# One static work order for another in a fused attention and feed-forward kernel

## The chip, the core and the metric

The program runs on one core of a Trainium2 chip. The metric is the device time of one execution in microseconds (us); smaller is better. The core has engines with instruction queues of their own: TensorE (PE, matmuls; its weight loads are shown as PEld), VectorE (DVE), ScalarE (ACT), GpSimd (POOL) and SyncE (SP). An engine takes its instructions strictly in the order in which the program lists them and waits where an input or a buffer is not ready; transfers are issued from the queues of POOL, SP and ACT and run on 16 shared DMA engines.

## What is computed

The reference, cut to what matters (8 batches, 12 heads, 448 positions, head size 64; 3584 tokens, model width 768, hidden width 2048):

```python
scores = np.matmul(q, k.transpose(0, 1, 3, 2)) / np.sqrt(64)
attn   = np.maximum(scores, 0.0) ** 2 / 448
x      = np.matmul(attn, v).transpose(0, 2, 1, 3).reshape(3584, 768)
h      = x @ w_in
out    = (0.5 * h * (1.0 + erf(h / np.sqrt(2)))) @ w_out
```

## The kernel before, in words

The work is cut into some 1480 operations, each a closure that emits the instructions of one engine. Attention is done batch by batch, in three groups of four heads. Per group of a batch the operations are:

- loads of q, k and v, cast to 16 bits on the way, issued by POOL (add_q, add_k, add_v, lines 546 to 577); the weights come the same way (add_win, add_wout). In the built program the loads of POOL take eight semaphores in turn, so a load is issued only when the eighth before it has landed;
- the transposes of q and k. Batches 0 and 1 do them on PE through PSUM (add_tk, add_tq, lines 600 and 625), and DVE or ACT copies the result out. From batch 2 on they are DMA transposes issued by SP (add_T_dma, lines 655 to 708; the instruction is on line 663), one for k and one for q of each group, and DVE or ACT then fills the other half of the q tile with two copies (fill_halves). SP's queue is in order, and it also issues the stores of the output;
- seven QK blocks (add_steps, line 752 for the matmuls): PE multiplies into one of three PSUM buffers, ACT or DVE takes the relu of it (lines 764 and 766), DVE squares it (line 773). In batch 0 a block is half as wide, and two go together;
- one AV (add_av, line 813), and two copies of its result x out of PSUM (line 514 on DVE, 516 on ACT).

Then follows the feed-forward part: the first product F1 (line 865, followed by the gelu on ACT, line 875) and the second (line 1182). Four batches' F1 and all of the second product are done in seven instead of eight block products, with sums formed on DVE; the F1 of that kind is line 1009. F1 of batch 0 needs the attention output of batch 0 and the weight block of its column. PE's queue weaves these products between the attention of later batches. At the end stands the last block of 128 output rows: its last piece of PSUM is filled in two parts of 256 and 128 columns, each with an addition on DVE (line 1216) and a store (line 1143) issued from the ACT and the SP queue.

A matmul of the QK and AV kind works on quarters of PE's array (64 by 64, four at a time), one of the feed-forward kind on the whole array (128 by 128). One QK block is four matmuls, an AV 28, an F1 word 6 (or 12 half as wide), a second product 8.

What order these operations have is not decided at run time. The string ORDER (lines 83 to 171) lists them all. A word is a letter for the engine (P for PE, A for ACT, D for DVE, G for POOL, S for SP) and the number of the operation; words of one letter, read in turn, are the queue of that engine. Z1024 and Z672 are matmuls on zeros that write to a scratch buffer. place() takes the words one by one:

```python
for word in ORDER.split():
    if word[0] == "Z":
        op, eng = next(fills), "PE"
    else:
        op, eng = self.open[int(word[1:])], names[word[0]]
```

and run() then emits the closures in that order, with waits wherever an operation needs the result or the buffer of another. The planner's estimates in the file no longer decide anything, since ORDER holds every operation.

POOL has gates besides: a tiny copy that reads a transposed q tile (add_gate, line 712; add_vgate, line 720) and so keeps all later loads of that queue back until that transpose has landed.

Words that matter below, with the size that lands in the core's memory:

| words | what |
|---|---|
| G0 G3, G1 G4 G7, G2 G5 G6 | batch 0: rest of k (224 KB each), rest of q (112, 112 and 336 KB), v (224 KB each) |
| G117 G118 G119, G121 G122 G123, G125 G126 G127 | batch 1: k, q, v of groups 0, 1, 2, 224 KB each |
| G8, G9 | w_in columns for F1 words m=0,1 and m=2,3: 384 KB each, three issues |
| G120, G124, G128 | w_in for m=4 to 7, 8 to 11, 12 to 15: 768 KB each, three issues |
| G238, G239, G241 | w_out: 1536 KB (one issue), 768 KB (two), 768 KB (two) |
| G147 G148, G150 G151, G153 G154 | batch 2: k and q of groups 0, 1, 2, 224 KB each |
| G149 G152 G155 | batch 2: v, 224 KB each |
| S228 S229, S231 S232, S234 S235 | batch 2: DMA transposes of k and q, of groups 0, 1, 2 |
| P99 | the last AV of batch 0 |
| P141, P143 | F1 of batch 0: m=0,1 and m=2,3 on the first half |
| P294 and P309 | a QK of batch 2, group 0 and group 1: the first of their groups in the order after |

Of the kernel before, what the change touches and what calls it, by code (L numbers as in the profile page):

```python
# [106 lines left out]
D452 P504 P539 P541 D458 A475 A505 A463 G422 A540 G424 D482 D506 A542 P489 P471 D464 G425 P513
D472 P543 P525 A514 D455 P477 D449 S407 A478 P468 A544 A469 D572 D490 A526 P507 P483 D479 D484
P545 S552 A508 A470 D485 G560 P519 S554 P501 A546 P486 P498 D502 S555 G563 D570 P521 A520 A487
P527 A522 A528 P529 S557 P549 A499 A530 D491 P533 P495 D553 A550 D488 A534 S445 D473 D556 P613  # L110
A496 D509 S558 D476 D614 P492 D493 P634 A494 A635 P616 D617 G426 D503 D571 P531 P523 P625 D500
A532 P628 P510 P535 D618 D626 A524 A511 A536 D497 D515 D573 A629 P547 G566 D512 A548 P576 P574
D615 D559 P646 P619 G561 A647 P516 S446 D575 G562 P622 D620 S714 G564 D577 A623 P640 G565 A517
D641 D624 P578 P580 A518 D627 A579 P537 A538 P637 D636 P610 D621 D648 D581 A611 D642 D630 P676
D638 P584 S715 D612 S717 P582 D585 G567 A677 A716 D583 G568 D639 P649 D592 P661 P631 S718 D590
A662 P586 D632 P643 D591 A650 P788 A633 D587 A644 G723 A789 P652 D663 A653 D651 P596 P670 P658
D719 P594 P673 D645 A671 S720 D654 A595 P655 D659 G726 S721 G569 G729 P667 D660 D597 D656 A674
D672 A668 P776 P598 P600 A657 S588 P664 A777 G724 D678 P779 D675 D601 A599 S845 D722 P797 D593
P602 D669 A798 A780 P604 D778 A665 D603 P785 P791 A786 A792 D666 D605 P839 P606 D840 G725 P679
P773 P800 D841 A774 D787 D607 P700 D680 A801 P712 G727 A681 A701 D781 D790 D733 P809 P782 S846  # L120
P833 A713 A783 P682 P688 D775 A683 A810 D793 G728 D784 D847 P686 S848 S849 G730 G731 G854 A834
P836 P821 D850 P794 A689 A822 D799 P806 D837 S851 A687 P830 P704 A795 A807 D735 D796 S852 A831
P696 P815 A705 A697 P803 D808 P812 A813 P692 P698 G857 D811 D802 A693 P710 D832 P824 A816 D804
D814 G732 A699 P896 A825 D805 D817 P818 D897 G860 G855 D823 P890 P827 A711 A819 P702 D891 D835
A828 G856 D829 A820 A703 P926 D838 S956 G858 P902 P884 A903 A885 D826 G859 D853 P694 A927 D734
P684 P923 D924 A685 P893 A894 P842 A695 P914 P887 P708 P690 A843 S957 A888 D958 A915 P947 D895
P917 A844 A709 D898 A691 S589 D892 G861 D886 D928 S608 P899 A948 A900 P706 A918 S609 S959 P737
D736 P920 D889 P908 D904 D901 P905 G862 A738 D921 D922 P938 S960 D906 A909 A707 P911 A912 D961
D916 P739 P935 A907 D913 D740 P974 P741 A939 A975 P992 A742 D925 P932 A936 D940 P743 D949 P745
D919 A993 D744 D910 P950 A933 D755 D746 P977 D753 P929 S962 D754 A951 P944 P747 A978 P749 A930  # L130
A945 A931 P1004 P1001 D952 S963 D934 A1005 D748 P941 P757 D937 A942 D750 P759 D946 S751 D979 D756
A1002 D943 G1481 D964 P968 A758 P980 P953 D1037 A981 D760 P983 P763 P761 D984 P971 A969 D970 D764
A954 P1007 D985 D976 A762 D1003 D1045 D1046 P767 A972 A955 G863 A1008 D768 P765 P965 P998 P995
A966 P868 P1022 D973 A999 D1006 D766 A869 D982 D967 S752 D1038 A996 A1023 P986 D1041 P989 D997
P872 P1025 D987 A990 A988 D1047 D994 P1016 A1026 P1031 P769 A1017 D991 D1009 A1032 P1019 D1000
P1010 D770 P1028 A1020 P1049 A1029 P1066 D1033 P1051 A1067 D864 P1068 D1040 D865 P1070 A1011 A1012
D1024 P1013 D1039 P870 A1071 D1048 A1050 D1069 A1014 D1052 D1117 P1053 D1042 P1072 A1054 D1044
P1055 D1073 P1057 P1074 D871 D1056 P1083 D866 S771 D1075 P1100 P1060 P874 A873 D1043 P1077 D1058
P1063 A1059 D1018 P1080 D1078 D1015 A1084 P1087 D1061 D1030 D1081 D1064 P876 D1021 A1101 P1085
A1088 P1102 D1027 A1065 D1103 A1082 P1104 P1034 D1086 D875 A1105 D1035 D1036 P1089 A1079 P1106  # L140
P1091 P1108 P1121 D1107 D1090 P1111 P1138 P1094 A1062 D1118 A1122 D1092 P878 D1112 A1093 D1095
D1109 D867 D877 D879 P1125 D1119 P1123 A1139 A1076 D1341 P1114 P1097 A1096 A1113 P1142 D1098 P1140
A1110 P880 D1115 D1124 P1155 A1099 A1126 D1120 D1141 A1116 P1172 A1143 P1144 D881 D1145 P1193
D1189 D1229 P1127 A1173 D1190 P1157 A1156 S772 P1174 D1191 D1175 P1149 P1195 P1178 A1194 D1150
D1128 P1176 D1158 D1342 P1132 D1133 P1161 P1159 P1129 D1179 P1146 A1160 D1162 D1192 D1196 P1197
P1183 A1177 P1163 P1166 D1130 P1135 D1164 P1169 D1167 A1131 D1147 A1148 D1136 P1199 S882 A1151
D1184 D1230 P1152 A1165 A1198 P1180 D1170 P1201 D1200 P1233 D1181 S883 D1153 P1250 A1251 D1231
A1234 P1186 D1187 P1235 P1252 D1343 D1232 D1202 A1185 D1236 A1182 A1154 A1188 P1241 P1203 A1137
A1168 D1253 A1134 P1258 P1256 A1171 D1204 D1209 P1205 D1257 D1206 P1254 D1210 P1239 P1213 P1215
D1212 A1214 D1259 D1240 D1216 P1264 D1211 P1244 P1261 D1262 D1245 D1242 S1207 P1219 P1217 D1220  # L150
P1267 A1218 D1265 P1247 P1223 P1221 D1248 D1224 P1284 D1344 A1268 P1269 D1222 D1270 P1225 A1285
P1237 P1286 D1301 A1266 P1288 D1226 P1273 P1271 P1305 A1255 S1208 A1238 D1287 D1274 D1306 P1345
D1302 A1289 P1290 A1272 D1291 P1275 P1362 D1276 D1303 P1278 A1260 P1309 P1295 D1296 P1307 D1279
P1292 A1346 D1308 D1293 P1347 P1364 D1348 D1310 P1281 P1298 P1351 D1282 S1227 A1277 A1363 D1299
# [1369 lines left out]
```

## Time and profile before

| | |
|---|---|
| time of three runs | 366.73, 366.67, 365.64 us; median 366.67 |
| span of the profiled execution, first to last instruction | 363.4 us |
| PE busy in that span | 355.2 us |
| DVE, ACT, POOL busy | 297.0, 216.4, 64.3 us |
| moved by DMA | 42.97 MB |

The profile is one execution. Its own time is its span; the median of the runs lies 3.3 us above it, which is what surrounds the first and the last instruction. A page shows the busy time of each engine, then the span in 40 slices with a digit for the busy tenths, then the DMA queues (q0 is POOL's, q1 SP's), the chain of work that ended last, and the costliest groups. Further views list instructions in order of time (timeline), busy time by stretches (windows) and groups by shape.

### The profile page before, as it was taken

The numbers are of one execution on the slowest core, as the hardware profiler recorded it, in microseconds if no ns is written. First come the engines' busy times: TensorE is split into PE (matmuls) and PEld (weight loads), VectorE is DVE, ScalarE is ACT, GpSimd is POOL, SyncE is SP. The second block draws the span as 40 slices with busy tenths as digits, with TensorE's granted clock in tenths as the row PEclk, the third lists the DMA queues.
The fourth block names the chain that finished last, engine by engine and source line by source line (L and its number), as shares of the span: only waits on it lengthen the run. The fifth ranks groups of instructions, "written<-read, shape, count | busy, mean of one in ns | idle before, by whom it ended". The sixth has DMA issues, their size and how long they took to land.

```text
span 363.4 us, 8571 instructions
## 1 busy us (share of the span) xinstructions
PE 355.2 (98%) x3589; PEld 224.7 (62%) x3589; DVE 297.0 (82%) x518; ACT 216.4 (60%) x345; POOL 64.3 (18%) x104
## 2 busy tenths in 40 slices
PE   8899999999999999999999999999999999999995
PEld 4566565455545455544445556988887788778663
DVE  3998886598988999999889999989788657656862
ACT  5997674688778649779898678346143244116200
POOL 8665700432401403224010000000000000000000
PEclk9999999999999999999999999999999999999999
DMA  9999999999999899999695211003002020302232
GB/s 176 200 201 204 201 205 180 178 187 178 168 169 176 142 144 169 213 161 188 128 196 78 88 45 43 2 3 88 1 2 87 18 73 0 87 5 85 88 88 87
DMA packets 72326, 42.97 MB, mean 118 GB/s; under 512 B 37984, under 2 KB 68960, under 8 KB 72288
## 3 DMA queue, kind: packets, MB, share of 16 engines
q0 software_dynamic: 32912, 22.47, 43.2%
q1 hardware_dynamic: 38736, 19.46, 26.4%
q8 instruction: 28, 0.46, 0.5%
q10 hardware_dynamic: 640, 0.51, 0.4%
q14 instruction: 10, 0.08, 0.1%
HBM read 45.61 MB, written 11.01 MB: 156 GB/s over the span
## 4 chain that ended last, share of the span: by engine, by line
PE 92%; ACT 3%; DVE 2%; DMA 1%; issue 0%; DVEq 0%
PE pso L1182 35%; PE psh L865 21%; PE pb L1009 18%; PE ps L752 10%; PE pav L813 8%; ACT a_sq L764 2%; DMA k<-in_k_dram 1%; DVE a_sq L773 1%; ACT qT L516 1%; DVE qT L514 0%; PE tp L608 0%; PE tp L636 0%; DVE a_sq L766 0%; DVE kT L514 0%; DVE xT L514 0%
## 5 line engine op out<-in xcount | busy, mean ns | idle before, releaser
L764 ACT ACTIVATE a_sq<-ps 128x896 bf16<-128x896 f32 (+1 forms) x133 | 116.1, 922 | 22.0 <-PE ps L752 21.5
L773 DVE TENSOR_TENSOR a_sq<-a_sq 128x896 bf16<-128x896 bf16 (+1 forms) x169 | 97.2, 614 | 3.0 <-ACT a_sq L764 2.5
L865 PE MATMUL psh<-xT,win_sb 128*128 128x448 bf16 (+1 forms) x420 | 77.2, 337 | 0.0
L1046 DVE TENSOR_TENSOR part<-pb,part 128x448 f32<-128x448 f32 x80 | 47.0, 618 | 18.1 <-PE pb L1009 16.5
L865 PEld LDWEIGHTS <-win_sb 128*128 128x128 bf16 x420 | 38.9, 98 | 36.0 <-issue 8.5
L1182 PEld LDWEIGHTS <-s_sb 128*128 128x128 bf16 x456 | 43.3, 98 | 28.9 <-issue 3.8
L752 PE MATMUL ps<-qT,kT 64*64 64x448 bf16 (+1 forms) x756 | 48.3, 337 | 1.7 <-ACT a_sq L764 1.0
L1182 PEld LDWEIGHTS <-h_sb 128*128 128x128 bf16 x336 | 31.9, 98 | 22.3 <-issue 3.8
L875 ACT ACTIVATE h_sb<-psh 128x448 bf16<-128x448 f32 x64 | 34.8, 551 | 18.2 <-PE psh L865 17.9
L766 DVE TENSOR_SCALAR a_sq<-ps 128x896 bf16<-128x896 f32 (+1 forms) x36 | 38.5, 1073 | 7.2 <-PE ps L752 6.7
L1182 PE MATMUL pso<-wout_sb,s_sb 128*128 128x384 bf16 (+2 forms) x232 | 41.1, 321 | 0.0
L1182 PE MATMUL pso<-wout_sb,h_sb 128*128 128x384 bf16 x224 | 41.0, 326 | 0.0
L1182 PE MATMUL pso<-t_sb,s_sb 128*128 128x384 bf16 x224 | 41.0, 326 | 0.0
L1009 PEld LDWEIGHTS <-win_sb 128*128 128x128 bf16 x384 | 36.8, 98 | 3.6 <-issue 0.7
L813 PE MATMUL pav<-a_sq,v_sb 64*64 64x448 bf16 (+1 forms) x756 | 36.5, 329 | 0.3 <-ACT a_sq L764 0.2
L1055 ACT ACTIVATE h_sb<-part 128x448 bf16<-128x448 f32 x48 | 24.7, 572 | 17.7 <-DVE part L1046 17.7
L752 PEld LDWEIGHTS <-kT 64*64 64x64 bf16 x756 | 19.0, 105 | 24.3 <-issue 18.3
L1216 DVE TENSOR_TENSOR osb<-pso,p_sb 128x384 f32<-128x384 f32 x42 | 23.3, 554 | 12.3 <-PE pso L1182 7.6
L1009 PEld LDWEIGHTS <-ws 128*128 128x128 bf16 x288 | 27.7, 98 | 1.3
L813 PEld LDWEIGHTS <-v_sb 64*64 64x64 bf16 x756 | 21.1, 107 | 11.4 <-issue 1.4
L1009 PE MATMUL pb<-xT,win_sb 128*128 128x224 bf16 x192 | 23.0, 259 | 0.0
L516 ACT COPY part<-pb 128x448 f32<-128x448 f32 x16 | 8.2, 531 | 24.7 <-PE pb L1009 24.7
(62 smaller groups left out, 316.1 us busy)
## 6 DMA issues: line engine op xcount, KB each, us to landing
nk<-in_k_dram POOLq DMA_DIRECT2D x23, 224.0 KB, 7.7
nq<-in_q_dram POOLq DMA_DIRECT2D x21, 224.0 KB, 8.7
v_sb<-in_v_dram POOLq DMA_DIRECT2D x5, 672.0 KB, 9.0
out_dram<-osb SPq DMA_DIRECT2D x7, 336.0 KB, 2.8
v_sb<-in_v_dram POOLq DMA_DIRECT2D x9, 224.0 KB, 7.9
out_dram<-osb SPq DMA_DIRECT2D x7, 288.0 KB, 2.9
out_dram<-osb SPq DMA_DIRECT2D x8, 240.0 KB, 3.0
win_sb<-in_moe_w_in_dram POOLq DMA_DIRECT2D x8, 192.0 KB, 8.7
```

The lines of the kernel that those rows point to most:

```text
L752: nc.tensor.matmul(ps[64 * j : 64 * j + 64, e, x * w : x * w + w], kT[r, g, i * 128 + 64 * j : i * 128 + 64 * j + 64], moving, start=True, ...
L764: A.activation(ar, ps, AF.Relu, scale=c_att)
L766: V.tensor_scalar(ar, ps, c_att, 0.0, op0=mybir.AluOpType.mult, op1=mybir.AluOpType.max,)
L773: V.tensor_mul(box["a2"][:, :, :used], ar, ar)
L813: nc.tensor.matmul(pav[0][o2 : o2 + 64, e, :w], vt[b][r, 2 * g + e, bass.ts(i, D)], box["a2"][r, y, o : o + w], start=(i == 0), stop=(i == ...
L865: nc.tensor.matmul(ph[:, x * n : x * n + n], win_sb[:, kd, bass.ts(m + x, 128)], xT[b][:, kd, c], start=(kd == 0), stop=(kd == KD - 1),)
L875: A.activation(h_ring()[:, m : m + nm, o + c.start : o + c.stop], box[0][:, :S].rearrange("p (x n) -> p x n", x=nm), AF.Gelu,)
L1009: nc.tensor.matmul(bank[name][:, y, z * HS : z * HS + HS], w[:, k, bass.ts(mm, 128)], right()[:, k], start=first and k == 0 and z == 0, st ...
L1046: V.tensor_add(get(to), ps(name), get(other))
L1055: A.activation(h_ring()[:, m : m + 2, o + half[c].start : o + half[c].stop], src().rearrange("p (x n) -> p x n", x=2), AF.Gelu,)
L1182: nc.tensor.matmul(box[bank][:, n0:n1], left()[:, kf], right()[:, kf, n0:n1], start=bool(need) and kf == 0, stop=kf == K2 - 1, skip_group_ ...
L1216: V.tensor_add(out()[:, n0:n1], box[bank][:, n0:n1], other()[:, n0:n1])
```

## The change

Only ORDER is replaced; every operation of the one list is in the other. 42 operations go from DVE to ACT and 40 from ACT to DVE (relus, copies out of PSUM, fills). All engines get another sequence: PE's from the fourth word on; POOL's from the eighth, up to the batch 3 loads; SP's within the transposes of batches 2 and 3. The list after has three lines fewer, so that line numbers after it are smaller by three.

On POOL, the loads of batch 2 (G147 to G155) come ahead of parts of the weights and of batch 1's v: the sequence is now ... G8 G126 G120 G124 G151 G148 G119 G128 G127 G147 G150 G9 G123 G238 G239 G154 G155 G241 G240 G153 ..., where it was ... G126 G5 G8 G122 G120 G124 G119 G128 G123 G9 G127 G239 G238 G241 G147 G148 G150 G151 G153 G154 .... On SP the six transposes of batch 2 come as S232 S229 S228 S235 S231 S234 instead of S228 S229 S231 S232 S234 S235. PE changes between the attention kind of matmul and the feed-forward kind 89 times instead of 103. Batch 2's first QK stands 14 F1 words after P99 instead of 27. The two parts of the last piece swap places: P1470 (128 columns) now comes ahead of P1469 (256 columns), while their stores keep the order S1476 (256 columns), S1477.

The diff, cut to the lines that are spoken of:

```diff
@@ -81,88 +81,85 @@
 
 
 ORDER = """
-G0 G1480 D13 A10 A16 P14 D15 G1 P11 D12 P17 P36 P33 D18 G3 P19 D20 P21 A37 D22 A34 P39 P42 G4 P23
-P51 D43 P25 P48 A40 P54 A52 D24 D26 G7 G118 A55 P66 D44 Z1024 Z672 P63 A67 D49 D35 D41 A64 P69 D53
-G2 P57 P27 D28 D65 P31 A58 D32 D38 D68 P75 P78 P131 P29 A70 D132 A76 G117 P102 G121 P45 D59 A79
-A103 G6 P129 P111 A112 P108 D71 G125 A109 P105 A46 D30 P133 D130 A134 D77 D106 D56 P72 P96 A47
-P159 A73 P137 D50 A97 D74 G126 A160 P174 P84 G5 P139 P60 D80 D138 A175 G8 G122 A85 D113 G120 P81
-D104 P156 D61 D62 G124 A82 D98 D110 D83 D86 G119 P93 P90 P141 D107 A94 P162 A157 P87 A91 G128 P114
-G123 A142 A163 A88 P135 D95 D140 D92 P99 D115 D89 A116 D100 P165 G9 A136 P171 P145 D166 A172 P195
-P180 G127 D101 D167 P198 P251 A146 P249 D173 D196 G239 A252 P253 A199 D158 G238 P222 A181 P213
-G241 D164 D161 A250 P168 A223 P243 G147 A254 D169 S228 A214 D176 D170 P257 P189 P177 P183 D190
-P219 D220 A244 A258 G148 A178 P263 A179 A264 P255 D184 D182 D191 G150 P186 D185 P207 G151 P192
-A256 P267 D224 D200 P265 A193 A268 D221 D194 P143 A266 G153 S229 D208 S231 P261 P204 A187 A144
-D215 A262 D209 P210 A205 P216 D197 S232 P247 D188 P259 A248 A211 A260 G154 D206 D217 D218 P201
-D212 D202 P225 G237 S234 P245 A203 A226 A227 A246 P366 P364 A367 G240 D380 G149 D388 A365 P368
-A369 P352 P372 A353 A373 P356 S235 D383 D381 G152 D384 G155 A357 G242 D387 D389 P378 A379 P348
-A349 D382 P354 D230 A355 G269 D385 D233 P370 A371 P362 P358 P291 A363 A292 P294 A295 P285 A359
-G270 D286 P360 S408 P279 A361 P276 D277 P309 P350 A280 A310 A351 P374 P282 D236 A375 G271 S409
-D296 D287 D281 P318 S411 A283 P288 P376 D289 D284 P392 P312 P300 A377 A319 D391 A313 D293 D278
-A393 A301 G272 D386 G273 P339 P394 P396 P315 G274 D390 D290 D395 A340 D316 P306 D302 G417 D317
...
-D1436 D1440 P1443 D1442 P1445 D1444 P1447 D1455 D1446 P1449 D1453 D1448 S1451 P1457 D1454 D1450
-S1452 P1459 D1456 D1458 P1461 D1460 P1463 D1462 S1473 P1465 D1464 P1467 D1466 S1474 P1469 D1468
-S1475 P1470 D1471 S1476 D1472 S1477
+G0 G1480 Z672 D13 P14 D15 A10 P11 D12 A16 P17 D18 P33 A34 P36 P42 D43 G1 P21 D22 G3 G4 G7 G118 G117
+P19 D20 P39 G2 G125 A37 D44 P23 D24 A40 D38 P54 A55 P51 A52 P25 D26 P48 D49 Z1024 P66 A67 G122 G6
+P27 D28 G121 G5 G8 P57 A58 P69 A70 D35 P31 P131 D32 P63 D50 P108 G126 A109 G120 D68 D132 D41 A64
+G124 P29 D30 P75 P129 D130 P102 P45 A76 P137 D53 A103 D59 D56 A46 A47 P111 P78 A112 A79 G151 G148
+P84 A85 P135 P174 A175 G119 D71 D65 P72 A73 A74 D138 P105 D110 D80 P133 D106 P96 A97 D77 P159 A160
+D86 P60 D61 P81 P90 D62 D134 A82 D83 G128 G127 P93 A94 P141 P156 D113 A91 A142 D107 P171 A172 D104
+P87 A88 A89 D92 P139 D98 P114 G147 S232 A157 S229 S228 D95 D136 D140 P99 D100 A115 A116 D161 A101
+P165 G150 G9 G123 P145 G238 G239 G154 D173 S235 S231 A166 P222 P183 D184 P162 A223 A163 D185 A146
+P249 P186 A250 P207 D176 A208 P168 D169 P255 A256 P257 A258 P253 A187 P204 A254 P213 A214 D164 D170
+D167 D158 P177 A178 G155 D224 D205 G241 D206 P216 G240 G153 A217 P180 S234 D181 A179 P251 A252 D218
+P198 A199 D188 D200 P219 P195 P243 G271 A244 P267 D196 D220 D221 A268 P263 A264 P210 A211 D212 P192
+P189 P265 P143 D197 A266 D182 D209 A144 P259 A190 D215 P247 A260 D193 D194 G269 G270 G242 P261 S409
+P225 G149 G237 A230 D191 A262 D226 A248 P294 A295 P201 D227 P291 A202 A203 P285 D380 A292 P245 A246
+P366 D388 A367 A286 P364 A365 D287 D381 P368 A369 P352 P372 A353 A373 P356 A357 D389 D391 D382 P378
+D233 A379 P348 A349 D296 P362 A363 P279 A280 P309 A310 D236 D383 G152 G272 G273 P276 A277 P354 P360
+A355 A361 P318 D384 D281 P282 P288 D283 D289 G274 P370 A371 D293 A319 P374 P312 A375 D278 D320 D284
+P300 A301 D302 P339 S411 D390 D290 A313 D314 P358 D386 A359 P350 A351 P376 A340 S408 S412 S414 P315
+P306 A307 P297 S415 P324 G417 G420 G275 D316 A377 P303 D410 A325 D311 P392 A393 P394 A298 G423 G418
+D308 G419 D387 D385 A304 P396 D395 D397 D317 P333 P336 A299 P330 D334 A337 P398 D399 P400 A331 D305
+D401 P402 P456 D403 S406 A413 D457 P342 D326 D427 A343 D332 P321 P327 A322 A323 S551 D428 A328 D344
+P447 D341 P404 P431 P453 D405 A448 D432 P450 A451 P465 A466 D335 A454 D458 P433 D429 D434 D467 D329
+G421 P435 A436 P437 D338 P462 D430 P459 A463 D460 D461 D438 P345 A346 P480 G422 D416 G424 G425 A347
...
+A1422 A1372 P1425 D1426 P1427 D1428 S1431 P1429 A1412 A1361 A1375 A1409 A1392 A1355 D1433 D1434
+D1430 P1437 A1438 D1435 P1439 D1436 P1441 D1440 D1442 P1443 D1444 S1432 P1445 D1446 P1447 D1453
+D1454 D1448 P1449 D1450 D1455 S1451 D1456 S1452 P1457 A1458 P1459 D1460 P1461 A1462 S1473 P1463
+P1465 D1464 P1467 D1466 P1470 D1472 D1468 S1474 S1475 P1469 D1471 S1476 S1477
 """
```

More of the change, by code (lines that the diff above doesn't have):

```diff
@@ L107 @@
[L107 to L154, printed above, removed]
@@ new lines @@
+P483 P439 P441 D449 A481 P471 D440 A484 D485 A472 D442 P489 S407 S552 A553 S554 D464 D452 S555 P513
+A514 D455 P443 D444 D490 D491 P539 P541 P477 D478 D479 G560 A540 P507 A508 P468 A542 P474 P504 A505
+A469 D556 A470 S557 S445 G563 D482 P545 A546 S558 D475 P525 A526 P486 D487 D488 P498 A499 D473 P501
+A502 P543 P519 D476 P495 A496 A520 P613 D572 D614 P492 A544 D493 D570 A494 D509 P634 D635 P616 A617
+P521 P549 G426 A522 A550 P625 D571 D626 G566 P510 A511 D506 P628 A629 D503 P529 A530 D512 P527 G561
@@ new lines @@
+A528 S446 G562 S714 S715 G564 S717 G565 S718 P533 P531 P646 G567 D627 D500 D515 A647 G568 A534 G723
+A532 D497 P619 D620 P516 P640 D517 D518 D621 D648 D615 P622 G726 P547 A548 A641 D716 D630 P523 A524
+A623 P535 A536 D636 P574 A575 P576 D573 P637 A638 D559 S720 P610 P673 P578 A674 D642 D577 D611 A579
+D624 P580 D581 P537 A538 P584 S721 A722 D639 P582 D612 P649 G569 G729 G724 P670 D618 D592 D585 D650
+A671 P631 A632 A633 P652 P643 D583 D651 D590 D591 P586 D587 P594 G725 P676 A653 D654 D675 P664 A644
@@ new lines @@
+D645 A595 P788 A665 P596 D789 D593 A677 P658 P667 A668 D659 P655 G727 P661 G728 D790 P776 A777 S588
+D669 D597 P598 D662 D663 P600 D672 D666 A656 A657 A599 A719 S845 S846 P602 D678 P785 A786 D601 D603
+P779 A780 D660 D778 P797 P604 A798 D605 S848 S849 P606 P839 G730 D787 P791 G731 A792 P679 A680 D607
+D840 P773 A774 P800 D793 A681 D801 D850 D775 P712 D802 G854 P700 A713 A701 P833 A834 P782 P809 D781
+D783 P682 A683 D784 P688 A689 A810 D733 D799 P686 A687 P836 D837 P821 A822 P794 A795 P806 A807 D823
@@ new lines @@
+D847 P830 D796 A831 D838 D832 P696 A697 P704 A705 P803 D735 P815 D816 D808 A804 P812 A813 P692 A693
+P698 P710 A711 P896 S851 S852 P824 D814 A825 A699 D805 D811 D817 P818 A819 D897 P827 A820 G857 G732
+D853 D828 P890 D835 A891 D892 P702 D841 A703 P902 P926 G860 G855 A927 D928 G856 D829 G858 P884 A903
+A885 G859 P684 P694 D826 D886 A685 P893 P923 A924 P842 D894 S956 S957 D895 P887 D888 A695 D904 A843
+A844 P899 A900 P708 P911 A709 P947 D889 A948 A912 P914 A915 D958 S589 S608 S609 S959 P690 P706 A707
@@ new lines @@
+D901 P917 P920 A921 S960 G861 G862 D898 D734 P905 A691 D918 D919 D925 P974 A975 D736 D976 P932 D913
+A906 D961 A907 P737 A738 A933 P739 D740 G1481 D934 D922 P938 A939 P908 A909 P935 A936 D910 P741 A742
+D916 P743 D744 P950 D951 D952 S962 P977 D949 A978 P929 P941 A942 D943 P944 A945 D979 A930 A931 P745
+D746 S963 A964 D940 P747 D748 S751 D937 P980 A981 D753 D754 P1001 A1002 P992 A993 P749 P757 A758
+D750 D755 D1003 D946 P759 P965 A966 P1004 D1005 P953 D954 D955 D760 P968 A969 D970 P989 A990 D991
@@ new lines @@
+P761 D982 P983 P971 G863 D1045 A762 P1028 A972 P763 D764 A984 D967 P868 D973 D756 D985 A1029 P767
+D1037 P995 P998 A996 D768 D869 D997 D1046 D1048 P986 A987 A988 D994 P1022 A1023 P765 D766 P872 A999
+D1000 D1006 D1024 P1007 A1008 D1009 D864 D865 P1025 A1026 S752 P1016 A1017 P769 S771 D770 P1031
+A1032 D1038 P1010 D1041 P1019 A1020 P1013 A1014 D1011 A1012 P870 D871 P1049 P1066 A1067 D1047 P1083
+D1040 D1044 A1050 P1051 D1052 D866 P1070 A1071 P1068 P1053 P1100 A1054 D1039 D1042 P1055 D1056 P1057
@@ new lines @@
+D1058 A1084 P1087 A1101 P1104 A1105 A1059 A873 D1069 A1088 P1060 D1043 P1074 D1018 P1072 D1027 D1073
+D1075 D867 D1061 A1062 A1076 P1063 D1064 P1085 P1102 D1086 P874 D875 P1077 P1080 D1081 P876 P1089
+D1103 A1082 P1091 P1108 P1106 D1090 P1094 D1092 A1093 D1078 A1079 D1119 P1121 D1107 D1109 A1122
+D1015 P1097 P1111 D1112 A1113 P1138 A1139 A1110 D1095 D877 D1117 P1114 S772 D1098 D1115 P1125 P1155
+P1172 D1021 A1156 D1030 P880 D881 D1231 P1142 D1033 D1229 A1116 P878 A1126 P1034 A1143 D1118 D1120
+A1173 P1123 D1124 P1140 D1141 A1035 D1230 D879 A1036 P1157 D1158 P1174 D1175 P1176 P1159 A1160 A1177
@@ new lines @@
+P1127 D1341 P1161 D1128 P1144 D1162 A1099 P1178 D1179 D1145 P1166 D1167 P1163 P1180 P1149 A1065
+P1183 D1181 A1096 D1189 P1186 P1193 S882 D1164 P1169 D1150 P1132 D1184 D1187 A1188 D1342 P1233 D1133
+D1191 P1250 A1251 A1134 D1170 P1129 P1146 A1234 A1185 D1232 P1235 P1252 A1171 D1147 A1148 P1152
+D1190 P1195 D1253 D1130 D1236 D1153 P1256 D1257 P1239 D1240 P1135 D1136 D1344 P1261 D1262 P1244
+D1245 A1194 D1196 P1241 P1258 D1259 P1254 P1267 P1197 A1198 D1242 P1264 P1247 P1199 D1265 P1284
+A1154 A1285 A1268 D1200 A1165 A1131 D1248 P1201 A1182 A1137 D1202 P1269 P1286 A1168 D1287 P1203
@@ new lines @@
+P1290 P1271 D1192 P1205 A1151 D1209 D1211 D1210 D1204 P1237 P1213 S883 S1207 D1206 D1214 P1215 P1217
+D1216 P1219 S1208 D1291 D1212 A1218 P1221 D1220 D1222 P1223 P1225 A1260 A1238 A1255 D1270 A1272
+P1288 A1289 D1224 S1227 D1226 P1295 P1273 P1275 P1292 A1246 D1301 D1296 P1345 P1362 A1346 D1274
+D1276 P1278 P1281 A1277 D1293 D1279 A1363 A1280 D1343 D1282 P1366 A1297 A1249 P1349 P1347 P1364
+D1348 P1298 P1351 D1303 P1305 A1306 D1365 P1368 D1299 A1300 D1302 D1304 D1352 P1353 P1370 P1356
+D1369 P1373 D1371 D1357 P1376 A1266 P1307 D1354 P1359 S1228 D1374 D1308 P1379 A1380 D1377 A1243
```

18 lines of the change are left out of this document (5 added, 13 removed).

## Prediction

> **What bounds the kernel now.** I read the page first, then the windows, then PE's timeline.
>
> ```profile
> span 363.4 us, 8571 instructions
> ...
> PE 355.2 (98%) x3589; PEld 224.7 (62%) x3589; DVE 297.0 (82%) x518; ACT 216.4 (60%) x345; POOL 64.3 (18%) x104
> ...
> PE 92%; ACT 3%; DVE 2%; DMA 1%; issue 0%; DVEq 0%
> ```
>
> ```profile
> 10.00:20.00 10.00, 8.57 (x224) 5.99 (x225) 9.97 (x19) 9.92 (x16) 5.84 (x9) 1.00 1.32 201
> ...
> 20.00:30.00 10.00, 9.29 (x230) 6.88 (x225) 9.01 (x20) 9.69 (x14) 5.71 (x9) 1.00 1.29 203
> 30.00:40.00 10.00, 10.00 (x108) 5.45 (x106) 7.67 (x13) 7.02 (x12) 7.25 (x12) 1.00 1.30 202
> ...
> 50.00:60.00 10.00, 10.00 (x101) 5.74 (x100) 7.97 (x11) 5.63 (x11) 0.73 (x1) 1.00 1.33 201
> ```
>
> The columns are stretch, length, then busy us of PE, PEld, DVE, ACT and POOL, clock, DMA share, GB/s. Two stages differ. Up to about 30 us DVE and ACT are both full and PE waits for them; after that PE has no gap, at full clock. So a new order can gain in two ways alone: a shorter opening, or less PE time per unit of work later. Any wait that it adds on PE after 30 us is paid in full, since no later idle time takes it up.
>
> A busy PE still spends time on something other than streaming:
>
> ```profile
> 39.84 2.44 PE L865 MATMUL psh<-xT,win_sb 128*128 128x448 bf16 x12
> 42.22 0.76 PE L752 MATMUL ps<-qT,kT 64*64 64x448 bf16 x12
> ...
> 94.35 0.76 PE L752 MATMUL ps<-qT,kT 64*64 64x448 bf16 x12
> 95.05 1.47 PE L1182 MATMUL pso<-wout_sb,s_sb 128*128 128x384 bf16 x8
> 96.36 1.46 PE L1182 MATMUL pso<-t_sb,s_sb 128*128 128x384 bf16 x8
> 97.75 0.38 PE L752 MATMUL ps<-qT,kT 64*64 64x448 bf16 x4
> 97.96 1.49 PE L813 MATMUL pav<-a_sq,v_sb 64*64 64x448 bf16 x28
> 99.29 0.36 PE L752 MATMUL ps<-qT,kT 64*64 64x448 bf16 x4
> 99.80 0.38 PE L752 MATMUL ps<-qT,kT 64*64 64x448 bf16 x4 [0.15 <-ACT a_sq L764]
> ```
>
> Read start to start. An AV takes 99.29 - 97.96 = 1.33 us, so four such matmuls 0.19. A second product takes 1.31 ahead of one of its kind (95.05 to 96.36) and 1.39 ahead of a QK (96.36 to 97.75): 0.08 for the change to quarter-array matmuls. Three QKs take 0.70 ahead of a product (94.35 to 95.05) where 3 x 0.19 = 0.57: 0.13 for the change back. I take **0.10 us per change of kind**. Two F1 words and one change take 2.38 (39.84 to 42.22), an F1 word 1.14.
>
> **The change, part by part.**
>
> *Fewer changes of kind.* 89 instead of 103: 14 x 0.10 = **-1.4 us**, after 24 us, where nothing but PE bounds; ends -1.1 (0.08) and -1.8 (0.13). [...]
>
> *The opening.* The PE words ahead of P99 are the same but for one QK of batch 1 (P162 before, P171 after), so the question is when P99 can start, and what DVE and ACT must do until then.
>
> ```profile
> L764 ACT ACTIVATE a_sq<-ps 128x896 bf16<-128x896 f32 x132 | 115.7, 925 | 21.9 <-PE ps L752 21.5
> L516 ACT CAST xT<-pav 128x224 bf16<-128x224 f32 x5 | 1.7, 361 | 0.1
> L516 ACT COPY kT<-tp 128x896 bf16<-128x896 bf16 x1 | 0.9, 906 | 0.0
> ...
> L514 DVE CAST xT<-pav 128x224 bf16<-128x224 f32 x7 | 2.6, 387 | 1.0 <-PE pav L813 1.0
> ```
>
> ```profile
> 7.54 0.62 DVE L514 COPY kT<-tp 128x896 bf16<-128x896 bf16 x1 [0.76 <-PE tp L608]
> ...
> 28.11 0.86 PE L813 MATMUL pav<-a_sq,v_sb 64*64 64x224 bf16 x28
> 28.81 0.55 PE L752 MATMUL ps<-qT,kT 64*64 64x448 bf16 x8
> ```
>
> Counting words to the last relu that P99 needs (A91 in both), ACT has one relu (0.925) and one k copy (0.906) less and one x copy (0.361) more: -1.47 us. To the last square (D92 before, D95 after) DVE has one x copy less: -0.39. DVE is the fuller one, so it decides: 0.39, and about 0.3 of the idle 0.76 at 7.54, which D43 now fills. I take **-0.65 us**; the ends are 0 (the saved time is lost in waits between the two) and -1.2 (0.39 + 0.76). The fill Z672 goes into the wait ahead of P14 and costs nothing there.
>
> *One stall.* The 0.15 us at 99.80 goes: **-0.15**; what is late next is below.
>
> *The end.* The 256-column piece now comes last.
>
> ```profile
> 357.82 1.48 PE L1182 MATMUL pso<-wout_sb,s_sb 128*128 128x256 bf16 x16
> ...
> 359.34 0.62 DVE L1216 TENSOR_TENSOR osb<-pso,osb 128x256 f32<-128x256 f32 x2 [0.76 <-PE pso L1182]
> ...
> 359.79 0.85 ACTq L1143 DMA_DIRECT2D out_dram<-osb  x2
> ```
>
> Before, the store of the 256 columns is issued at 359.79 while PE's second part is still being added, and the small store follows it. After, S1476 waits for an addition that starts only when PE has ended, and S1477 is queued behind it: between 0.1 (the longer addition alone) and 0.5 later (issue after issue); I take **+0.3**.
>
> *The loads and DMA transposes.* This is what decides. POOL's loads saturate the DMA engines, and the new order asks for batch 2 earlier.
>
> ```profile
> nk<-in_k_dram POOLq DMA_DIRECT2D x23, 224.0 KB, 7.7
> ```
>
> ```profile
> q0 software_dynamic: 2536, 2.01, 128.2%
> ...
> q0 software_dynamic: 1103, 0.69, 135.8%
> ...
> kT<-nk SPq DMA_TRANSPOSE x2, 6.7
> qT<-nq SPq DMA_TRANSPOSE x1, 6.7
> ...
> q0 software_dynamic: 338, 0.17, 48.7%
> ...
> q1 hardware_dynamic: 4174, 1.03, 105.6%
> ...
> kT<-nk SPq DMA_TRANSPOSE x1, 10.9
> qT<-nq SPq DMA_TRANSPOSE x1, 8.0
> ...
> q0 software_dynamic: 635, 0.38, 88.1%
> q1 hardware_dynamic: 647, 0.17, 44.0%
> ...
> kT<-nk SPq DMA_TRANSPOSE x1, 2.9
> ```
>
> ```profile
> 57.55 1.31 SPq L663 DMA_TRANSPOSE kT<-nk  x1
> ...
> 68.30 0.76 PE L752 MATMUL ps<-qT,kT 64*64 64x448 bf16 x12
> ```
>
> The rows of the DMA view (queue, packets, MB, share; then issues with the median us to landing) are, in turn, of the stretches 20 to 30, 57.55 to 61, 61 to 64, 64 to 69, 126.3 to 130.5, 131 to 134 and 176.5 to 180. The loads move 2.01 MB in 10 us, 196 KB per us, which no order changes. The first transposes are issued at 57.55, but until 61 only q0 moves. Its last 0.17 MB run out by 64; 11184 KB are listed up to and with batch 2's q and k, so I set their end at 61.5. The order after lists 10192 KB up to G154: it cannot be through before 61.5 - 992/196 = 56.4. A transpose alone moves 224 KB in 1.1 us (1.03 MB in 5 us), and three stand ahead: 59.7. S235 needs that load, and S231 stands **behind S235 in SP's queue** though its own load is long there; one issue is 1.31, so S231 is issued at 61.0 at the earliest. To its landing it takes 2.9 us with the queues empty, but 6.7 to 10.9 with loads ahead of it, as here (G155, G241). I take the middle of the three loaded rows, 8.0: it lands at 69.0; the ends are 63.9 and 71.9.
>
> When does PE ask for it? P99's QK starts at 28.81 - 0.65 = 28.15. From there to P294 stand 14 F1 words (16.0 us), 17 QKs (3.2), two AVs (2.7) and 12 changes (1.2): 51.2. On to P309 come ten F1 words, an AV, four QKs and two changes (13.7): 64.9. So P309 waits 69.0 - 64.9 = **+4.1 us**; ends 0 and 7. Behind it stands all of PE's queue. The load of P143 (G9: 42.4, with two transposes 44.6) is due at about 45, and S228 (load through at 39.3, with two transposes 41.5, then 8.0: 49.5) is due at 51.2; both just hold.
>
> Sum: -1.4 - 0.65 - 0.15 + 0.3 + 4.1 = +2.2. The profiled 363.4 becomes 365.6, and with the 3.3 us around it, 366.67 becomes **368.9 us**.
>
> **The rivals.**
>
> *Transposes share at once (faster).* If a transpose's packets enter among the loads as soon as it is issued, S231 lands within 3.9 us of 61.0 and P309 waits for nothing: 366.67 - 1.9 = 364.8. The point of decision is that 3.9. For it: once both move (131 to 134), they do so packet for packet, 647 to 635, and 2.9 us has been seen. Against it: with loads ahead no row is under 6.7. [...] I give 0.25.
>
> *Transposes wait for all loads queued ahead.* The row of 57.55 to 61 reads like that too: nothing moved until the loads ran out. Then S228, issued at about 43 with up to eight loads ahead (3136 KB, 16 us) and three transposes' own 3.3, lands at 62 instead of 51.2: +10.8, about 375.5. Against it: at 131 they shared before the loads were through. 0.12.
>
> *The order buys nothing.* The two engines lose in mutual waits what the opening saves and P309 waits about 2 us: within 0.3%, 366 to 367.7. 0.13.
>
> **How the numbers follow.** The forecast has 0.50, with its own range 367.8 to 371.9 (3.0 more when the landing is at its late end, 1.1 less when it takes 6.7). About 0.3%, 1.1 us, is what a measurement here can tell from no change: below 365.57 lies the first rival and little else, 0.26; within, 0.13; above, 0.61. The range reaches from 364.5, just under the fast rival, to 373.5; about 0.1 is left out on either side.
>
> **What would show it.** After: an idle gap of PE ahead of its first QK of batch 2's group 1, released by a DMA into kT, with S231 issued at 61 or later and some 7 us to land; no such gap of over 1 us would make the forecast wrong, and one ahead of P294 of ten would be the second rival. P99's successor near 28.15 shows the opening, PE rows from 100 to 340 without gaps the changes of kind, and the last addition 0.1 to 0.5 us later against PE's end shows the tail. A gap that ACT or DVE ends between 100 and 340 us would be a cost that I have set at nothing.

## The result and the profile of the changed kernel

| | before | changed |
|---|---|---|
| time, median of 4 runs, us | 366.17 (365.64 to 366.73) | 394.82 (392.64 to 395.88) |
| span of the profiled execution, us | 363.4 | 394.1 |

The ratio is 1.0784 with a 95% interval of 1.0744 to 1.0824: the new order costs 28.6 us, far beyond the range on record. Every run on record with both figures takes some 1.8 us more than its span (395.88 against 394.1). So the 3.3 us between 363.4 and 366.67, put ahead of the prediction as what surrounds the first and the last instruction, also holds a difference between executions. This moves nothing in the forecast, which adds its 2.2 us to the median. The profiled execution of the changed kernel is the longest of its four (395.88 us).

From the page of the changed kernel, its length, its engines and its chain of waits:

```profile
span 394.1 us, 8584 instructions
...
PE 362.1 (92%) x3589; PEld 226.3 (57%) x3589; DVE 300.3 (76%) x513; ACT 218.6 (55%) x350; POOL 64.8 (16%) x104
...
PE 68%; DMA 16%; DVE 10%; issue 2%; POOL 1%; ACT 1%; DVEq 0%; POOLq 0%; ACTq 0%
```

PE has the same 3589 matmuls, but it is no longer the chain: 16% of it are transfers and 10% DVE, where there were 1 and 2. The windows of the changed kernel say where (columns as in the prediction; the clock is the share of TensorE's full speed that was granted):

```profile
70.00:80.00 10.00, 7.20 (x43) 3.02 (x44) 5.29 (x8) 3.62 (x7) 5.93 (x10) 0.83 1.04 143
90.00:97.00 7.00, 4.26 (x27) 1.93 (x25) 6.14 (x10) 4.07 (x6) 3.61 (x7) 0.76 1.03 182
100.00:235.00 135.00, 135.00 (x1375) 70.70 (x1368) 127.97 (x214) 105.32 (x153) 19.67 (x32) 1.00 0.80 134
235.00:390.00 155.00, 139.56 (x1135) 106.97 (x1132) 102.49 (x181) 45.84 (x94) 0.00 (x0) 1.00 0.14 41
```

There are two places, with 135 us without a gap between them. One is the stretch up to 100 us, where the clock falls as well; the other begins at 235 us, where PE stands 15.4 of 155 us, at full clock and with next to no transfers.

**The early place.** PE's timeline of the changed kernel:

```profile
48.59 4.63 PE L862 MATMUL psh<-xT,win_sb 128*128 128x224 bf16 x35 [1.30 <-DMA win_sb<-in_moe_w_in_dram]
...
55.22 0.38 PE L749 MATMUL ps<-qT,kT 64*64 64x448 bf16 x4 [0.55 <-DMA kT<-nk]
...
72.80 0.69 PE L749 MATMUL ps<-qT,kT 64*64 64x448 bf16 x8 [3.71 <-DVE qT L511]
73.42 3.96 PE L862 MATMUL psh<-xT,win_sb 128*128 128x448 bf16 x12
...
94.30 2.72 PE L1179 MATMUL pso<-wout_sb,s_sb 128*128 128x384 bf16 x8 [2.74 <-DVE osb L1213]
```

The row at 72.80 begins with P309, the first QK of batch 2's group 1, which the prediction named. It needs S231, the transpose of its k. First SP's queue, where S231 is the first of the two in the second row; then the load G154, from the chain of work that ended last (start and length):

```profile
64.58 1.22 SPq L660 DMA_TRANSPOSE qT<-nq  x1
65.84 6.79 SPq L660 DMA_TRANSPOSE kT<-nk  x2
```

```profile
45.28 19.28 DMA nq<-in_q_dram
```

G154 lands at 64.56, S235 is issued behind it at 64.58 and S231 behind that at 65.84; S231 lands at 72.76. The profile names DVE's fill D236 for this wait, since that one ended at 72.79; but D236 stands behind P309 in the list, and e5 below takes P309's wait away while D236 comes later still. The four waits are 8.3 us. After the two long ones PE also runs slowly: two F1 words take 3.96 us instead of 2.44, and a second product 2.72 instead of 1.47, together 2.8 us. What DVE waited for between 50 and 95 us, from the view of waits (total, times, longest):

```profile
DVE qT L511 <- DMA qT<-nq: 7.6, 2, 3.8
DVE t_sb L1116 <- DMA wout_sb<-in_moe_w_out_dram: 5.7, 1, 5.7
```

So DVE, whose queue is in order too, stood behind two fills (D236 and D410) whose transposes had not landed, and behind the first sum on w_out (D380). The second fill is what made the product at 94.30 late.

**The late place.** The block products (line 1006) of the changed kernel after 235 us, by group:

```profile
L1006 PE MATMUL pb<-xs,win_sb 128*128 128x224 bf16 x192 | 22.8, 259 | 5.3 <-DVE part L1043 5.0
...
L1006 PE MATMUL pb<-xT,win_sb 128*128 128x224 bf16 x192 | 22.0, 259 | 2.9 <-ACT part L513 2.5 <-DVE part L1043 0.5
L1006 PE MATMUL pb<-xs,ws 128*128 128x224 bf16 x192 | 21.5, 259 | 3.4 <-DVE part L1043 3.4
...
L1006 PE MATMUL pb<-xT,ws 128*128 128x224 bf16 x96 | 11.6, 259 | 3.4 <-DVE part L1043 3.4
```

All of the waits but the 0.4 us ahead of the last product, 15.0 us, stand ahead of block products. Nearly all of them are ended by the sums and copies that read an earlier product out of PSUM. In the kernel before the same stretch has none:

```profile
235.00:359.00 124.00, 124.00 (x1026) 96.63 (x1024) 89.81 (x163) 39.17 (x82) 0.00 (x0) 1.00 0.17 48
```

DVE is idle a third of the late stretch in the changed kernel, so its throughput does not bound it. Either PE and DVE pay back there what DVE lost early, or the late order has waits of its own.

### The profile page after: what moved, and what is told of

It is laid out like the page before. It is cut to its first block, busy times and chain, and to the rows that moved or that the text cites. A ratio compares the mean times of both kernels' runs of the same rounds, so it can differ in the third digit from the quotient of the medians.

```text
span 394.1 us, 8584 instructions
## 1 busy us (share of the span) xinstructions
PE 362.1 (92%) x3589; PEld 226.3 (57%) x3589; DVE 300.3 (76%) x513; ACT 218.6 (55%) x350; POOL 64.8 (16%) x104
## 4 chain that ended last, share of the span: by engine, by line
PE 68%; DMA 16%; DVE 10%; issue 2%; POOL 1%; ACT 1%; DVEq 0%; POOLq 0%; ACTq 0%
PE pso L1179 31%; PE pb L1006 14%; PE psh L862 12%; DMA nq<-in_q_dram 9%; PE ps L749 6%; PE pav L810 5%; DVE part L1043 5%; DMA nk<-in_k_dram 3%; DMA v_sb<-in_v_dram 2%; DMA qT<-nq 2%; DVE a_sq L770 2%; DVE osb L1213 1%; DVE s_sb L1160 1%; DVE xs L973 1%; ACT part L513 1%
## 5 line engine op out<-in xcount | busy, mean ns | idle before, releaser
L761 ACT ACTIVATE a_sq<-ps 128x896 bf16<-128x896 f32 (+1 forms) x128 | 111.9, 925 | 30.7 <-PE ps L749 30.6
L862 PE MATMUL psh<-xT,win_sb 128*128 128x448 bf16 (+1 forms) x420 | 79.1, 342 | 1.5 <-DMA win_sb<-in_moe_w_in_dram 1.3
L1043 DVE TENSOR_TENSOR part<-pb,part 128x448 f32<-128x448 f32 x80 | 48.0, 621 | 25.4 <-PE pb L1006 24.3
L763 DVE TENSOR_SCALAR a_sq<-ps 128x896 bf16<-128x896 f32 (+1 forms) x41 | 43.9, 1076 | 7.8 <-PE ps L749 7.4
L1179 PE MATMUL pso<-wout_sb,s_sb 128*128 128x384 bf16 (+2 forms) x232 | 42.5, 328 | 3.1 <-DVE osb L1213 3.1
L1052 ACT ACTIVATE h_sb<-part 128x448 bf16<-128x448 f32 x48 | 25.2, 573 | 24.7 <-DVE part L1043 21.9
L1006 PE MATMUL pb<-xs,win_sb 128*128 128x224 bf16 x192 | 22.8, 259 | 5.3 <-DVE part L1043 5.0
L1006 PE MATMUL pb<-xs,ws 128*128 128x224 bf16 x192 | 21.5, 259 | 3.4 <-DVE part L1043 3.4
```

The source lines that it names most:

```text
L761: A.activation(ar, ps, AF.Relu, scale=c_att)
L763: V.tensor_scalar(ar, ps, c_att, 0.0, op0=mybir.AluOpType.mult, op1=mybir.AluOpType.max,)
L862: nc.tensor.matmul(ph[:, x * n : x * n + n], win_sb[:, kd, bass.ts(m + x, 128)], xT[b][:, kd, c], start=(kd == 0), stop=(kd == KD - 1),)
L1006: nc.tensor.matmul(bank[name][:, y, z * HS : z * HS + HS], w[:, k, bass.ts(mm, 128)], right()[:, k], start=first and k == 0 and z == 0, st ...
L1043: V.tensor_add(get(to), ps(name), get(other))
L1052: A.activation(h_ring()[:, m : m + 2, o + half[c].start : o + half[c].stop], src().rearrange("p (x n) -> p x n", x=2), AF.Gelu,)
```

## The experiments

### Which part of the order costs what

**e1_early_part** and **e2_late_part** splice the two orders at about 204 us. The operations are the same in both, so a prefix of one order can be followed by what is left of the other (the edit in short; words are compared by their number, since 82 of them change their engine):

```diff
-ORDER = changed
+ORDER = changed[:900] + [w for w in before if number(w) not in numbers(changed[:900])]   # e1
+ORDER = before[:940] + [w for w in changed if number(w) not in numbers(before[:940])]    # e2
```

> The first 900 words of the changed order, then every operation that is left in the order of the kernel before: the opening and batch 2 to about 204 us as in the changed kernel, the late feed-forward part as before. Theory A (two separate losses): of the 28.4 us that the change costs, about 15 to 18 are the waits of PE ahead of the block products of line 1006 after 235 us (5.3 + 2.9 + 3.4 + 3.4 us in the groups of the changed kernel, none before), and they come from the late order alone; the rest, about 11, is lost ahead of 100 us. So this kernel should take 366.4 + 9 to 13, 375 to 379 us, and show no wait ahead of the block products. Rival B (one loss: DVE falls behind early, where it stands behind fills and weight sums whose transfers have not landed, and PE meets that arrears only after 235 us): nearly the whole loss stays, 390 to 395 us, with the same waits late.

> The mirror image: the first 940 words of the order before (to about 204 us), then every operation that is left in the order of the changed kernel. Theory A: 366.4 + 15 to 19, 381 to 386 us, with some 15 us of waits ahead of the block products and none earlier. Rival B: the early arrears are not there, so nothing is to be paid: 366 to 368 us.

Measured: e1 374.62 us, 1.023 of the kernel before (1.0186 to 1.0273), +8.7; e2 387.83 us, 1.0586 (1.0557 to 1.0615), +21.9. Together 30.6, against 28.6 for the whole change: two separate losses. Of e2's, 1.4 us are two waits of PE where the orders are joined (0.58 at 209.34, 0.81 at 210.53). Rival B is out: in e1 no block product waits. The groups of e2 after 200 us show it best:

```profile
L1009 PE MATMUL pb<-xs,win_sb 128*128 128x224 bf16 x192 | 22.8, 259 | 5.3 <-DVE part L1046 5.2
L1009 PE MATMUL pb<-xT,win_sb 128*128 128x224 bf16 x192 | 22.0, 259 | 2.9 <-ACT part L516 2.5 <-DVE part L1046 0.5
L1009 PE MATMUL pb<-xs,ws 128*128 128x224 bf16 x192 | 21.5, 259 | 3.4 <-DVE part L1046 3.4
L1009 PE MATMUL pb<-xT,ws 128*128 128x224 bf16 x96 | 11.6, 259 | 3.4 <-DVE part L1046 3.4
```

They are the waits of the changed kernel to a tenth, after an opening that had none to pass on. A delay handed down from the opening could not repeat them so exactly. Theory A was right on the place and missed both ranges, e1 by 0.4 us and e2 by 1.8. It had the late loss too small (15 to 19 us) because it took the idle column; that names only part of it, as the next runs show start to start.

### What the late order waits for

**e3_changed_apart** keeps the changed order and makes the two halves of a `pb` tile independent; `pb` is the PSUM tile that the block products write, and its halves are `[:, 0]` and `[:, 1]`. **e4_late_part_apart** does so with the order of e2.

```diff
+        def apart(name, i):
+            i = i.ins
+            seen = bank.setdefault(("seen", name), [])
+            for yy, j in seen:
+                if yy != y and j.engine != i.engine:
+                    tc.declare_no_dep(i, j, reason="other PSUM bank")
+            seen.append((y, i))
...
-                        nc.tensor.matmul(
+                        apart(name, nc.tensor.matmul(
                             bank[name][:, y, z * HS : z * HS + HS],
...
-                    V.tensor_add(get(to), ps(name), get(other))
+                    apart(name, V.tensor_add(get(to), ps(name), get(other)))
```

The copy and the gelu that read `pb` directly are wrapped likewise.

> The changed kernel with its own order, but the two halves of a pb tile, which lie in two PSUM banks, no longer count as dependent on each other: a product into one half doesn't wait until DVE or ACT has read the other half. Nothing else differs, and no data is shared between the halves. Theory A with this cause (the late order lets one half follow the other more closely, and the program makes a product wait for the reading of the other half): the late waits go, 394.8 - 15 to 18.5, 376 to 380 us. Rival C (the late waits are those of the data, a product that needs the sum just before it, or the buffer itself): 392 to 395 us. Rival B: 392 to 395 us as well.

> The order of e2 (before to about 204 us, then as changed) with the halves apart as in e3. Theory A with the halves as cause: within 2 us of the kernel before, 365.5 to 368.5 us. Rival C: 381 to 386 us as e2.

Measured: e3 373.2 us, 1.0195 (1.0165 to 1.0226), 21.6 less than the changed kernel; e4 367.67, 1.0048 (1.0031 to 1.0064), 20.2 less than e2. Rival C is out as well. The gain of e3 is 2.8 us beyond the range of theory A, for the same reason as in e2. The block products of e3 show no wait in any of their four groups, of which this is one:

```profile
L1014 PE MATMUL pb<-xs,win_sb 128*128 128x224 bf16 x192 | 21.8, 259 | 0.0
```

The timeline of the changed kernel around one such product, and then that of e3:

```profile
236.89 0.74 PE L1006 MATMUL pb<-xs,ws 128*128 128x224 bf16 x6
237.54 0.74 PE L1006 MATMUL pb<-xT,win_sb 128*128 128x224 bf16 x6
...
238.42 0.62 DVE L1043 TENSOR_TENSOR part<-pb,part 128x448 f32<-128x448 f32 x1
...
239.10 0.74 PE L1006 MATMUL pb<-xs,ws 128*128 128x224 bf16 x6 [0.82 <-DVE part L1043]
```

```profile
233.46 0.74 PE L1014 MATMUL pb<-xs,ws 128*128 128x224 bf16 x6
234.03 0.74 PE L1014 MATMUL pb<-xT,win_sb 128*128 128x224 bf16 x6
...
234.61 0.74 PE L1014 MATMUL pb<-xs,ws 128*128 128x224 bf16 x6
...
234.98 0.61 DVE L1051 TENSOR_TENSOR part<-pb,part 128x448 f32<-128x448 f32 x1
```

The first row is P1051, which writes one half of bank `b`; the last PE row is P1068, which writes the other half. In the changed kernel P1068 starts when DVE has read P1051's half (238.42 to 239.04). In e3 it starts 1.15 us after P1051, before that reading has even begun. The data never asked for the wait: the halves share no element, and P1068 needs nothing of the sum. The program orders them because both belong to one tile. From the first block product to the last product of the kernel PE takes 153.82 us in the changed kernel (235.17 to 388.99) and 134.68 in e3 (231.73 to 366.41), with the same order: 19.1 us, of which the idle column names 15.4.

**e7_before_apart** is the control: the order before, with the same edit.

> The kernel before, its order untouched, with the halves of a pb tile apart as in e3. Its PE has no gap of over 0.2 us after 30 us, so no theory expects anything: 366 us within 0.3%. It is the control for e3 and e4: if it were several us faster, the halves would be a cost of both orders and not of the late part of the new one.

Measured: 366.4 us, 1.001 (0.9997 to 1.0023). The rule was there before and cost nothing. The two lists show the difference. In the changed one the sum D1052, which reads P1051's half, stands ahead of P1068, so that P1068 waits for it; in the one before, P1068 follows P1051 directly on PE and D1052 stands behind both, so that it is the sum that waits. Counted over the 112 block products of each list, 17 of the changed order stand only one or two words of PE behind a product of the tile's other half whose reading is listed ahead of them; in the order before, 1 does.

### What is left: the stretch up to 100 us

**e5_k_first** exchanges two words of e3's order on SP; **e6_mended** makes four more moves. The edit of e5:

```diff
-... G154 D173 S235 S231 A166 ...
+... G154 D173 S231 S235 A166 ...
```

> e3 (changed order, halves apart) with one more edit: S231, the transpose of k of batch 2's group 1, stands ahead of S235 in SP's queue instead of behind it. What is left of the loss in e3 (7.3 us) has one large wait, 3.44 us ahead of P309 at 72.24, with the next words slowed by a lower granted clock (0.91 over 60 to 80 us). Theory D (S231 is late because S235 stands ahead of it and waits for the load G154): the wait goes and the clock stays up, 373.2 - 3.4 - about 1.5, 368 to 370 us. Rival E (k's transpose lands as late wherever it is issued, because its packets wait for the loads): 372.5 to 374 us, the wait still ended at about 72.

> e5 with four more words moved, one for each wait that is left in e3: G147 ahead of G127 and G9 ahead of G150 on POOL (for the 0.56 us ahead of the first QK of batch 2 and the 0.79 ahead of the F1 word at 48.29), D410 (a fill that waits for a transpose of batch 3) behind D397 on DVE (for the 1.25 us at 92.01), and P1470 with D1472 behind P1469 again (for the 0.38 at the end). If these waits were what is left, 368 to 370 of e5 minus 2.5 to 3, that is 365.5 to 367 us, about the kernel before or a little under it: 14 changes of kind at 0.09 are 1.3 us to gain, the opening loses 0.6. If the landings move with the loads so that another wait takes their place, 368 to 371 us.

Measured: e5 375.24 us, 1.0266 (1.0236 to 1.0295); e6 375.19, 1.0259 (1.0239 to 1.028). Both expectations were wrong on the time, and e5 was right on its mechanism. S231 was now issued at 45.5, and P309, at 69.99, has no wait ahead of it. But the next wait took its place; DVE, then PE, in e5:

```profile
75.95 0.79 DVE L514 COPY qT<-qT 64x896 bf16<-64x896 bf16 x2 [5.95 <-DMA qT<-nq]
```

```profile
80.31 0.59 PE L752 MATMUL ps<-qT,kT 64*64 64x448 bf16 x4 [4.33 <-DVE a_sq L766]
```

D236 waits for S235, S235 for its load G154, and that load is through at 66.4, no earlier than with S231 behind it (64.7 in e3). In e6 it was alike: P309 waits 0.50 us, but DVE stands 8.24 us at the first sum on w_out (D380) and 7.48 at D236, and PE 6.44 at 81.17.

**e9_b2_first** takes e6 and puts that load ahead of w_out's; on DVE, D233 goes ahead of D380.

```diff
-... G238 G239 G154 ... G241 ... G240 G153 ...
+... G154 G153 G238 G239 ... G241 ... G240 ...
```

> e6 with the loads of batch 2's group 2 (G154, G153) ahead of the three loads of w_out (G238, G239, G241) on POOL, and the fill D233 ahead of the first sum on w_out (D380) on DVE. In e6 and e5 the wait ahead of P309 was gone, but DVE then stood 6 to 8 us at the fill D236, until S235 had landed (its load G154 is through at 66), and PE waited 6.4 us for DVE at 81. Theory F (what is left of the opening's loss is only that batch 2's loads land too late for an order that asks for them 13 us earlier): D236 has its data by about 60, the wait at 81 shrinks to 0 to 3 us, total 369 to 372. If the loss only moves on, to the sums on w_out whose loads now land 2 to 3 us later: 373 to 376.

Measured: 373.62 us, 1.0226 (1.0195 to 1.0258): the second outcome. D236 no longer waits, but now w_out is late, and DVE stands at D380 for longer than it stood at both in e5 (5.65 and 5.95 us):

```profile
71.69 0.96 DVE L1129 TENSOR_TENSOR t_sb<-wout_sb 128x1536 bf16<-128x1536 bf16 x1 [14.51 <-DMA wout_sb<-in_moe_w_out_dram]
```

**e10_no_wout** takes bytes away instead of moving them; **e11_before_no_wout** is its control, and **e12_no_wout_trace** its trace.

```diff
             nc.gpsimd.dma_start(nk[b][:, 2 * g0 : 2 * g1], kv_view(k, b, g0, g1))
+            if (b, g0) == (2, 2):
+                for x in range(4):
+                    nc.gpsimd.memset(wout_sb[:, 4 * x : 4 * x + 4], 0.0)
...
-        nc.gpsimd.dma_start(wout_sb[:, kf, c], w[:, kf, c])
+        pass
```

> e3 (changed order, halves apart) without the loads of w_out: 3072 KB of transfers are left out, and POOL fills the tile with zeros after its last load of batch 2, so the output is zeros. Everything else is as in e3. Theory F (the opening's loss of e3, about 7 us, is transfer time: the new order asks for batch 2 before the bytes ahead of it can have landed): G154 lands some 10 us earlier than 64.7, the waits of DVE and PE between 55 and 95 us go, and e3's 373.2 becomes 366 to 368. Rival (the loss lies in how the transposes and their queues are ordered, not in the bytes): 370 us or more.

> The control for e10: the order before, halves apart, and the same loads left out and zeros in their place. PE has no gap there to lose, so 366 us within 0.5% by every theory; e10 is to be compared with this run.

> The kernel of e10 once more, for its trace alone, since the execution that was profiled there ran at a mean granted clock of 0.66. Theory F: no wait of PE above 1 us between 50 and 100 us, DVE not waiting for a DMA into qT for more than 1 us, and the loads of batch 2 landed by about 57.

Measured: e10 366.58 us, 1.0031 (1.0006 to 1.0056), 6.6 less than e3; e11 365.92, 0.9997 (0.998 to 1.0014); e12 366.6. In the windows of e12 PE has no gap where e3 lost its time:

```profile
60.00:80.00 20.00, 20.00 (x155) 9.76 (x156) 16.44 (x25) 14.15 (x23) 6.63 (x13) 1.00 1.13 161
80.00:100.00 20.00, 20.00 (x196) 10.94 (x192) 18.74 (x33) 14.21 (x21) 4.02 (x6) 1.00 1.06 177
```

In e12 G154 lands at 51.78 instead of 64.56, 12.8 us earlier; the 2304 KB of w_out listed ahead of it are 11.8 us at the 196 KB per us of the prediction. So the early loss is, in the main, transfer time: the order asks for batch 2 and the weights sooner than the bytes can land. In the four arrangements tried (e3, e5, e6, e9) the loss moved between them and none was free of it; that none could be is not shown. Nor does e10 part the bytes from what goes with them: five issues in POOL's queue, and DVE's wait for w_out itself.

### The price of a change of kind

**e8_more_changes** is the order before with 12 exchanges such as this one on PE:

```diff
-... P513 ... P543 ...
+... P543 ... P513 ...
```

> The kernel before with 12 pairs of neighbouring words of PE's queue exchanged between 100 and 215 us (F1 F1 A A becomes F1 A F1 A), so that PE changes its kind 24 times more; the other queues keep their order. By the price of the prediction, 0.10 us for a change, 366 + 2.4 = 368.4 us, with 0 to 0.6 more if a word that moves has to wait. [...] If a change costs nothing that the end sees, 366.

Measured: 369.01 us, 1.0085 (1.007 to 1.0099), +3.1 for 24 more changes: 0.13 for one, 0.11 to 0.15 by the interval, 0.12 without the one wait of 0.27 us that came in at 113.27. The price of the prediction, 0.10, was a little low; its upper end, 0.13, was met. The measured interval, 368.5 to 369.5 us, leaves out the 366 of a change that costs nothing.

## Where the prediction was right and where it failed

- **The sum has no term for the late order.** This is the step that failed. "A gap that ACT or DVE ends between 100 and 340 us would be a cost that I have set at nothing": it was 19 to 22 us (e2 +21.9, e3 -21.6). The prediction took PE's later time as streaming plus changes of kind. It counted what is issued and when transfers land, but did not set each block product of the new order against the reading of its tile ahead of it. Without this loss the same order takes 373.2 us (e3), at the far end of the stated range.
- **P309's wait had the right mechanism, and its size is luck.** Predicted 4.1 us; measured 3.71. The landing came 3.8 us later than predicted (72.76 against 69.0) and PE 4.2 us later (69.1 against 64.9), and the two errors cancel. The transpose was issued at 65.84 (at the earliest 61.0) and took 6.9 us (8.0). PE was held up by the waits at 48.59 and 55.22 (1.85 us) and by a QK after P99 that started 1.26 us later than predicted; the rest of the 4.2 lies in the words between. The load that decides it, G154, landed at 64.56, against "59.7". The term that was mis-sized is "A transpose alone moves 224 KB in 1.1 us"; its price to the loads is below.
- **What stands behind the same landings was left out.** The prediction followed PE's queue behind P309, not DVE's behind D236, D410 and D380. From there came 2.74 us at 94.30, and the lower clock after both gaps cost 2.8. The whole early loss was +8.7 (e1) or +7.3 (e3), where the prediction had +4.1 less 2.2.
- **The load of P143 and S228 did not "just hold"**: 1.30 and 0.55 us.
- **Fewer changes of kind** were priced nearly right (e8: 0.13 for 0.10). The gain does not show in the time: with the halves apart and w_out left out, the new order takes 366.58 us and its control 365.92 (e10 and e11), with intervals that touch. e12 names what stands against the 1.4 us: 1.36 us at 48.41, 0.29 at 54.78 and 0.38 at the end.
- **The opening** went the way that was predicted, but its size is not settled. The first transposes of PE started at 5.10 us in the profile of before and at 5.80 in that of the changed kernel, but also at 5.81 and 5.82 in e7 and e2 with the order before. Among the executions at full clock that start at 5.8, the QK after P99 comes at 29.29 to 30.33 in four with the old opening (e2, e7, e8, e11), and at 29.13 to 29.86 in six with the new one (after, e1, e3, e5, e6, e12): 0.5 earlier on average, with ranges that overlap; predicted was 0.65.
- **The end** cost 0.38, near the 0.3, but elsewhere: PE's last word waits until DVE has read the other part of its tile. The time from PE's end to the end of the span is 4.1 us in both.
- **The rivals.** Sharing at once did not happen: S232 was issued at 33.35, and up to 37 us only the loads moved; from 37 to 40 both queues did (0.34 MB of loads, 0.08 of transposes). S232, S229 and S228 took 10.7 to 13.8 us under loads. The 6.7 us of the prediction, under which it saw no row, is a median: one of the two transposes behind it, issued at 60.60, took 5.95. Waiting for all queued loads did not either: S228 landed at 55.2, not 62.

## What to carry to other kernels

When a static order is changed, look at what each instruction waits for in the built program, not only at the data it needs: a wait on a tile's other half cost nothing in one order (e7) and 20 us in another (e3, e4). A replay of measured landings did not hold once the order of the transfers changed (G154 landed at 64.56, against 59.7); where the transfers were the limit here, moving a load or a wait handed the loss to the next in line (e5, e6 and e9 took 373.62 to 375.24 us, against 373.2 in e3). Follow every in-order queue behind a late landing, not only the one that bounds the kernel, and try the halves of an order by splicing it with the old one.
